# A side tile of dead scratch buffers for the weights between two attention layers

## The chip, the cores and the metric

The kernel runs on one core of one Trainium2 chip. The metric is the device time of one launch in microseconds, the median of several runs. Operand types are bf16, with f32 sums.

## The reference

One token is decoded for each of four sequences, through four layers: attention, gated linear unit (GLU), the same attention again, the same GLU again. The second pass uses the same caches and weights as the first.

```python
x = A_x                                             # [4, 1, 512]
x = x + _A_ref(_layernorm(x), k_cache, v_cache, wq, wo)
x = x + _B_ref(_layernorm(x), w_gate, w_up, w_down)
x = x + _A_ref(_layernorm(x), k_cache, v_cache, wq, wo)
x = x + _B_ref(_layernorm(x), w_gate, w_up, w_down)

# _A_ref: 32 query heads, 8 KV heads, Dh = 128; the window is the last 2048 keys (W = 8192 // 4)
q = (x @ wq)                                        # wq [512, 4096]
p = softmax(q k^T * Dh ** -0.5)
out = (p v).reshape(B, 1, 4096) @ wo                # wo [4096, 512]

# _B_ref: F = 1792
out = (sigmoid(x @ w_gate) * (x @ w_up)) @ w_down
```

The window's K and V are 16 MiB each, wq and wo 4 MiB each, the three GLU matrices 1.75 MiB each.

## The kernel before

**Space.** SBUF holds an arena of 50 slots of 128 x 2048 bf16 (512 KB a slot). Two slots are a tile: 1 MB, which holds one KV head of two sequences. The first 32 slots hold all of K and stay for both attention layers. The other 18 slots are nine tiles for V, wq, wo and the GLU weights. Beside the arena lie scratch buffers, each a tensor of its own: `prow` (the scores' exponentials P, 512 bf16), `ebuf` (P transposed, 512 f32, in halves for even and odd units, tokens `("e", 0)` and `("e", 1)`), `qh` and `qbd` (q, and q spread into blocks for the score products), `mxt`, `rinv`, `onb`, `onp`, and small constants and masks.

**Units.** An attention layer is eight units, one for each KV head h: scores (L872, L883), softmax (L893 to L915, exponentials on ScalarE), P turned by a permutation product and a VectorE transposition (`turn_p`, L922), PV (L960 in the first layer, L1041 in the second), and the output product with wo. The first layer goes through h = 0 to 7 and also transposes each K tile in place (L854); the second goes through h = 7 to 0.

**What is kept between the layers.** The second layer needs V again. V tiles are named (h, bp), where bp is the pair of sequences, and a V tile has two halves. Tile (7, 1) and tile (6, 1) stay in the arena (`stay`, L1427). Tile (7, 0) is moved to four PSUM banks (`stash`) and comes back into a free tile (`load_stash`). Of tile (6, 0) the second half stays (`KEPT`, `keep_half`, L626); its first half is loaded again for the second layer. Everything else of V is loaded again.

**The change of layers.** Between the two attention layers the GLU weights (12 loads) and wq again (8 half tiles) pass through six half-tile homes while K and the kept V stay in place. The homes are written down with the loads: `GB` is a free tile (two homes), `Y` the tile of V (7, 0) after its stash (two homes), `Z` the first half of V (7, 1)'s tile, whose content waits in PSUM meanwhile (`stash_half`, `unstash_half`), and `GA` the first half of V (6, 0)'s tile. A home is free when what was in it has been read. The second layer's wq goes in the order i = 1 (q heads of h = 4 to 7), then i = 0, four chunks each; the homes of the last two chunks of i = 0 later serve as scratch (`wide_buffers`).

```python
load_half(("wq", c, k, i), wq_d[:, c, i * SLOT:(i + 1) * SLOT], "bw_4k", SLOT,
          (((Y, 1), (GB, 0), (GB, 1), (GA, 0)), ((GB, 0), (GB, 1), (GA, 0), (Y, 0)))[i][c])
```

**Order.** All loads are issued by SyncE (SP) from one list, `loads`, in the list's order (helper `dma`, L395; all loads have line L398). A load waits on SP until the engines that use its buffer have finished, so a waiting load also holds those behind it. The work of each engine is put in order by a planner (`_schedule`) from estimated costs, and the dependencies are tokens, turned into semaphore waits by `_assign_sync`. From the first GLU's end on, TensorE's order is the program order (`P.chain = True`).

Names and lines for later steps: `load_half` L487, `bounds_of` L516 (rows of w_down in one load), `load_wq` L522, `load_glu` L554, `load_v` L609, `q_mms` L784 (q products, L795), `q_turn` L803 (writes all of `ebuf` and half of `qh`), `attn_first` L1171, `glu` L1305 (gate and up products L1342, first w_down products L1408, last ones L1383).

Of the kernel before, what the change touches and what calls it, by code (L numbers as in the profile page):

```python
# [6 lines left out]
F32 = mybir.dt.float32  # L7
# [271 lines left out]
def build(nc, A_x, A_k, A_v, A_wq, A_wo, B_wg, B_wu, B_wd, out, cfg=None):  # L279
# [42 lines left out]
    with es:  # L322
# [4 lines left out]
        prow = sb("prow", [128, 512], BF16)  # L327
        ebuf = sb("ebuf", [128, 512], F32)
        qbd = sb("qbd", [128, 2 * NB * 4 * NR], BF16)
        qh = sb("qh", [128, 2 * 64], BF16)  # L330
        eyew = sb("eyew", [128, 224], BF16)
        ones_f = sb("ones_f", [128, 32], F32)
        perm = sb("perm", [128, 128], BF16)
        sel_f = sb("sel_f", [128, NR], F32)
        sel_b = sb("sel_b", [128, NR], BF16)
        s3 = sb("s3", [128, 2 * 3], BF16)
        sres = sb("sres", [128, 2], F32)
        sel_r = sb("sel_r", [128, 2 * REP], F32)
        maskr = sb("maskr", [128, 32], F32)
        mxt = sb("mxt", [128, 2 * 32], F32)  # L340
        nmax = sb("nmax", [128, 6], F32)
        msk_s = sb("msk_s", [128, 32], BF16)
        msk_m = sb("msk_m", [128, 2], BF16)
        psm = sb("psm", [128, 2], F32)
# [4 lines left out]
        maskp = sb("maskp", [128, REP], F32)  # L349
        msks = sb("msks", [128, 22], F32)  # L350
# [4 lines left out]
        lnr = sb("lnr", [128, 2 * NB], F32)  # L355
        lnd = sb("lnd", [128, NB], F32)
        lnv = sb("lnv", [128, NB], F32)
        inv_d = sb("inv_d", [128, 1], F32)
        xn = sb("xn", [128, NX], BF16)
        hT = sb("hT", [128, NFC * NB], BF16)  # L360
        x_nat = prow[0:NB, 0:D]
        eg = qbd[:, 0:2 * NFC * NB].bitcast(F32)
        ident = ebuf[:, 0:64].bitcast(BF16)
        ps = es.enter_context(nc.psum_tensor("ps", [128, 8, 512], F32))
# [14 lines left out]

        def slot_ap(s):  # L380
            return arena[:, s * SLOT:(s + 1) * SLOT]

# [37 lines left out]
        GA = ("V", HKV - 2, 0, 0)  # L420
        KEPT = ("kept",)
        GB = ("pair",)
        base = {}
# [10 lines left out]
        def take_load():  # L434
# [9 lines left out]
            if name in (Y, Z, GA, GB):  # L444
                base[name] = s
# [41 lines left out]
        def load_half(name, src, rate, size, where_):  # L487
            left[name] = 1
            homes[name] = [where_]
            on_free[name] = lambda s: hfree.add(s)  # L490

            def emit(s):
                dma(str(name), slot_ap(s)[:, 0:size], src, w=[("slot", s)], rate=rate)
            loads.append((name, emit))
# [21 lines left out]
        def bounds_of(k):  # L516

            return [(a, min(NFC, a + 4)) for a in range(0, NFC, 4)] if k < NG else bounds[:-1] + [(bounds[-1][0], NFC - 2), (NFC - 2, NFC)]
# [3 lines left out]
        def load_wq(k):  # L522
# [3 lines left out]
            else:  # L526
                for i in (1, 0):
                    for c in range(NC):
                        load_half(("wq", c, k, i), wq_d[:, c, i * SLOT:(i + 1) * SLOT], "bw_4k", SLOT,
                                  (((Y, 1), (GB, 0), (GB, 1), (GA, 0)), ((GB, 0), (GB, 1), (GA, 0), (Y, 0)))[i][c])  # L530
# [23 lines left out]
        def load_glu(k):  # L554
            for nm, src in (("wg", wg_d), ("wu", wu_d)):
                if k == 0:
                    for c in range(NC):
                        load_half((nm, c, k), src[:, c, :], "bw_3k", F,
                                  (((GB, 0), (GB, 1), (GA, 0), (Y, 0)), ((Y, 1), (Z, 0), (GB, 0), (GB, 1)))[nm == "wu"][c])
# [3 lines left out]
            for (a, b) in bounds_of(k):  # L563
                if k == 0:
                    load_half(("wd", a, k), wd_d[:, a:b, :].rearrange("p k n -> p (k n)"), "bw_4k", (b - a) * D,
                              ((GA, 0), (Y, 0), (Y, 1), (Z, 0))[a // 4])
# [42 lines left out]
        def load_v(h, bp, k, n_use):  # L609
            name = ("V", h, bp, k)  # L610
            tiles = {(HKV - 2, 0): ((Y, 0),), (HKV - 3, 1): ((Y, 1), (GB, 0))}.get((h, bp)) if k else None
            if tiles is not None:
# [5 lines left out]
                if len(tiles) == 1:  # L618
                    halves[h, bp].append((KEPT, 0))
# [6 lines left out]
        def keep_half(s):  # L626
            hfree.add(s)
            where[KEPT] = s + 1
            left[KEPT] = 2
        on_free[GA] = keep_half  # L630

        P.op("gpsimd", "ones", 200.0, lambda g: g.memset(ones_f[:], 1.0), w=[("ones_f",)])
        P.op("gpsimd", "ident_b", 300.0,
# [9 lines left out]
        for jh in range(2):  # L643
            for bp in range(2):
                for i in range(2):
# [7 lines left out]
                         r=[("ones_f",), ("perm",)], w=[("perm", jh, bp, i)])  # L653
# [5 lines left out]
             r=[("ones_f",)], w=[("msk_s",)])  # L659
# [4 lines left out]
             r=[("ones_f",)], w=[("msk_m",)])  # L664
        P.op("vector", "sel_f", 200.0,
             lambda v: v.tensor_reduce(sel_f[:, :], perm[:, :].rearrange("p (g x) -> p x g", x=NR), AXX, ALU.add),
             r=perms, w=[("sel_f",)])
        P.op("gpsimd", "sel_b", 200.0, lambda g: g.tensor_copy(sel_b[:, :], sel_f[:, :]),
             r=[("sel_f",)], w=[("sel_b",)])
# [867 lines left out]
```

## Time and profile before

| What | Value |
|---|---|
| median of 3 runs | 178.61 us (178.54 to 178.78) |
| span of the profiled execution | 177.03 us |
| PE, DVE, ACT, POOL busy | 58%, 59%, 18%, 12% of the span |
| loads | 70.26 MB from HBM |
| DMA engines' time on them | 97.4% of 16 engines' span |
| rate, 12 to 92 us | 420 GB/s |
| rate, 104 to 118 us (GLU weights) | 404 GB/s |
| rate, 122 to 124 us (wq of the second layer) | 350 GB/s |
| second layer's first scores | from 126.2 us |
| last load lands | 174.2 us |

The profiled execution's own time is its span; what the timed runs have beyond it lies around the program's instructions. In the profile's pages PE is TensorE's matmul, PEld its weight load, DVE VectorE, ACT ScalarE, POOL GpSimd and SPq the queue of SyncE. A load is recorded with its issue and its landing; the trace also has the landing on each of the 16 DMA engines. Times are microseconds from the span's start.

### The profile page before, as it was taken

Reading aid. Unit: us, or ns where it says so; the run is one execution under the profiler, and the core shown is the slowest. Engines: PE = TensorE matmul, PEld = TensorE weight load, DVE = VectorE, ACT = ScalarE, POOL = GpSimd, SP = SyncE. Lnnn points to the kernel's source line nnn. Section 1 sums busy time; section 2 is a strip of 40 time slices with the busy share of each in tenths; the row PEclk is TensorE's granted clock in tenths of the full one; section 3 lists DMA queues with packets and bytes.
Section 4 is the critical chain, followed back from the end, with each engine's and each line's share of the span. In section 5 each row is a group of like instructions: output and inputs, shape, how many; then the busy total and the mean of one; then the engine's idle time right before and its main releaser. Section 6 shows DMA issues by size and latency. Waiting matters only on the chain.

```text
span 177.0 us, 3893 instructions
## 1 busy us (share of the span) xinstructions
PE 102.3 (58%) x1641; PEld 55.0 (31%) x1653; DVE 104.6 (59%) x256; ACT 32.7 (18%) x87; POOL 21.6 (12%) x88
## 2 busy tenths in 40 slices
PE   0536236382842634607418866456886999776663
PEld 0203112241431431603404852052323444435322
DVE  7307997838477375594383772304299999742351
ACT  2002031312030210300301101000043365430011
POOL 6100010101010100100100100000011454342000
PEclk9999999999999999999999999999999999975555
DMA  6999999999999999999999999999999999999980
GB/s 179 418 429 428 420 422 416 416 420 426 411 414 429 415 422 418 415 420 426 411 420 428 400 403 403 409 401 387 404 429 409 420 418 422 413 417 405 413 351 28
DMA packets 12882, 70.52 MB, mean 398 GB/s; under 512 B 1336, under 2 KB 1344, under 8 KB 6720
## 3 DMA queue, kind: packets, MB, share of 16 engines
q1 hardware_dynamic: 12856, 70.26, 97.4%
q8 instruction: 13, 0.21, 0.5%
q14 instruction: 5, 0.04, 0.1%
q10 hardware_dynamic: 8, 0.00, 0.0%
HBM read 70.26 MB, written 0.00 MB: 397 GB/s over the span
## 4 chain that ended last, share of the span: by engine, by line
DMA 38%; DVE 32%; PE 18%; issue 4%; SPq 4%; ACT 2%; DVEq 0%; ACTq 0%
DMA arena<-in_B_w_down_dram 15%; DMA arena<-in_A_v_cache_dram 15%; DVE arena L854 11%; PE ps L883 7%; DVE nmax L896 5%; DMA arena<-in_B_w_gate_dram 4%; DMA arena<-in_A_wq_dram 4%; SPq L398 4%; PE ps L973 3%; PE ps L872 2%; DVE nmax L900 2%; DVE mxt L904 2%; DVE ebuf L931 2%; PE ps L1162 2%; DVE arena L1064 2%
## 5 line engine op out<-in xcount | busy, mean ns | idle before, releaser
L854 DVE STREAM_TRANSPOSE arena<-arena 128x1024 f32<-128x1024 f32 x32 | 37.0, 1202 | 0.0
L883 PE MATMUL ps<-arena,qbd 128*32 128x512 bf16 x256 | 25.6, 537 | 0.0
L896 DVE TENSOR_REDUCE nmax<-ps 128x1 f32<-128x512 f32 x16 | 10.8, 675 | 19.4 <-PE ps L883 19.3
L973 PE MATMUL ps<-ebuf,arena 128*128 128x8 bf16 x576 | 17.7, 168 | 7.5 <-DMA arena<-in_A_v_cache_dram 4.4
L872 PE MATMUL ps<-msk_m,msk_s 128*32 128x512 bf16 x64 | 8.6, 526 | 23.1 <-DVE arena L854 21.8
L973 PEld LDWEIGHTS ps<-ebuf,arena 128*128 128x128 bf16 x576 | 16.8, 104 | 9.5 <-DMA arena<-in_A_v_cache_dram 5.5
L911 ACT ACTIVATE prow<-ps,nmax 128x512 bf16<-128x512 f32 x16 | 11.0, 687 | 35.1 <-DVE nmax L908 29.5
L847 ACT CAST qbd<-ps 128x256 bf16<-128x256 f32 x16 | 5.9, 370 | 45.0 <-PE ps L883 35.1
L940 POOL CAST s<-psm 128x1 bf16<-128x1 f32 x9 | 1.7, 187 | 84.0 <-ACT prow L911 84.0
L883 PEld LDWEIGHTS ps<-arena,qbd 128*32 128x32 bf16 x256 | 8.4, 121 | 10.4 <-issue 7.7
L795 PE MATMUL ps<-arena,xn 128*4 128x512 bf16 x64 | 8.5, 572 | 4.9 <-DMA arena<-in_A_wq_dram 4.4
L926 ACT CAST prow<-ps 128x512 bf16<-128x512 f32 x16 | 9.4, 585 | 9.9 <-PE ps L973 2.1
L1342 PE MATMUL ps<-arena,xn 128*4 128x448 bf16 x64 | 7.7, 547 | 4.2 <-DMA arena<-in_B_w_up_dram 1.9
L931 DVE STREAM_TRANSPOSE ebuf<-prow 128x256 f32<-128x256 f32 x16 | 7.0, 435 | 3.8 <-ACT prow L926 3.7
L872 PEld LDWEIGHTS ps<-msk_m,msk_s 128*32 128x32 bf16 x64 | 1.7, 98 | 24.1 <-DVE arena L854 22.7
L773 ACT ACTIVATE lnv<-ps 128x4 f32<-128x4 f32 x4 | 0.7, 173 | 41.0 <-PE ps L769 41.0
L1055 PE MATMUL ps<-arena,ebuf 128*32 128x512 bf16 x112 | 7.9, 405 | 0.2 <-DVE nmax L908 0.2
L842 PE MATMUL ps<-qh,eyew 32*128 32x64 bf16 x64 | 5.6, 217 | 3.7 <-ACT qbd L847 2.4
L807 DVE STREAM_TRANSPOSE ebuf<-ps 128x512 f32<-128x512 f32 x3 | 2.1, 717 | 9.4 <-PE ps L795 9.3
L1351 DVE STREAM_TRANSPOSE ebuf<-ps 128x448 f32<-128x448 f32 x4 | 2.6, 650 | 7.1 <-PE ps L1342 7.1
L1162 PE MATMUL ps<-onp,arena 128*128 128x16 bf16 x144 | 5.3, 175 | 2.5 <-DVE onp L996 2.2
L981 DVE TENSOR_TENSOR onb<-ps,rinv 128x16 bf16<-128x16 f32 x9 | 1.7, 185 | 8.3 <-PE ps L973 8.1
(112 smaller groups left out, 132.2 us busy)
## 6 DMA issues: line engine op xcount, KB each, us to landing
arena<-in_A_v_cache_dram SPq DMA_DIRECT2D x27, 1024.0 KB, 22.4
arena<-in_A_k_cache_dram SPq DMA_DIRECT2D x16, 1024.0 KB, 25.1
arena<-in_A_wq_dram SPq DMA_DIRECT2D x4, 1024.0 KB, 8.0
arena<-in_A_wq_dram SPq DMA_DIRECT2D x8, 512.0 KB, 6.2
arena<-in_A_wo_dram SPq DMA_DIRECT2D x3, 1024.0 KB, 26.2
arena<-in_B_w_down_dram SPq DMA_DIRECT2D x4, 512.0 KB, 6.4
arena<-in_B_w_gate_dram SPq DMA_DIRECT2D x4, 448.0 KB, 8.3
arena<-in_B_w_up_dram SPq DMA_DIRECT2D x4, 448.0 KB, 6.2
```

Source lines behind the costliest of these rows:

```text
L795: last = pe.matmul(ps[32 * hh:32 * hh + NB, qb, :], xn[:, c * NB:(c + 1) * NB], src[:, o + hh * 512:o + (hh + 1) * 512], start=(c == 0), s ...
L854: P.op("vector", "T%d_%d" % (h, t), c_dve(1024), lambda v, v32=v32: v.transpose(v32, v32), r=[("slot", 4 * h + t)], w=[("slot", 4 * h + t)])
L872: last = pe.matmul(ps[32 * gi:32 * gi + 32, bank, :], msk_s[:, :], msk_m[:, :].unsqueeze(1).broadcast_to([128, 256, 2]), start=True, stop= ...
L883: last = pe.matmul(ps[32 * gi:32 * gi + 32, bank, :], qbd[:, q0:q0 + 32], kt[:, cp // 2, cp % 2, jh * NJ:(jh + 1) * NJ, :], start=False, s ...
L896: lambda v: v.tensor_reduce(nmax[:, k2:k2 + 1], ps[:, bank, :], AXX, ALU.max),
L911: lambda a: a.activation(prow[:, :].rearrange("p (m x t) -> p m x t", x=32, t=2), ps[:, bank, :].rearrange("p (m t x) -> p m x t", x=32, t ...
L926: P.op("scalar", "pc" + tag, c_act(512), lambda a: a.copy(prow[:, :], ps[:, pb, :]), r=[("ppb", pb)], w=[("prow",)], banks=(pb,))
L931: P.op("vector", "pt" + tag, c_dve(256), lambda v: v.transpose(et, prow[:, :].bitcast(F32)), r=[("prow",)], w=[("e", k2)])
L973: last = pe.matmul(ps[:, ob, bp * 8:bp * 8 + 8], src[:, j * 128:(j + 1) * 128], ev[:, j % 2, j % 16 // 2, x0:x0 + 8], start=(j == 0), stop ...
L1055: last = pe.matmul(ps[32 * g:32 * g + 32, ob, :], ew[:, g, mq, t], src.rearrange("p (m t d) -> p t m d", t=2, d=128)[:, t], start=(n == 0) ...
L1162: last = pe.matmul(ps[:, WB, c * NR:(c + 1) * NR], tile_ap(s)[:, o + r_ * D + c * 128:o + r_ * D + (c + 1) * 128], ov[:, r_ * NR:(r_ + 1) ...
L1342: last = pe.matmul(ps[32 * g:32 * g + NB, gub[n], 0:NF], xn[:, c * NB:(c + 1) * NB], slot_ap(s)[:, g * NF:(g + 1) * NF], start=(c == 0), s ...
```

## The change

The scratch buffers `prow`, `qbd`, `qh`, `mxt` and `ebuf` become parts of one tensor, `side`, of 2560 bf16 columns. Its first 2048 columns are a half-tile home: P, q, q blocks and mxt in the first 1536 columns, and the first half of `ebuf` in the last 512. This home, `SP`, takes the place of `GA` between the layers. `stok` gives a load of it, and a product that reads it, the tokens of every buffer that lies in it; with loads of up to 1536 columns `ebuf` is left out. It is handed over in unit 6 of the first layer (`give(SIDE)`).

V (6, 0) now stays whole, so its first half is not loaded again. The homes of the other weights are shifted: wq's third chunk of i = 1 and one w_gate chunk go to `SP`, and wq's last chunk of i = 0 goes to Y's first half, where the V half used to go. w_down of the first GLU comes in loads of 3, 4, 4 and 3 rows, so that its first fits in 1536 columns. To make room, `hT` moves into `rinv`, `eg` into `onp`, two constants into `ebuf`, and the small tensors are packed into one; `one`, a single column of ones, is new.

```diff
-        prow = sb("prow", [128, 512], BF16)
-        ebuf = sb("ebuf", [128, 512], F32)
-        qbd = sb("qbd", [128, 2 * NB * 4 * NR], BF16)
-        qh = sb("qh", [128, 2 * 64], BF16)
+        side = sb("side", [128, 1536 + 1024], BF16)
+        prow, qbd, qh = side[:, 0:512], side[:, 512:512 + 2 * NB * 4 * NR], side[:, 1024:1024 + 2 * 64]
+        mxt = side[:, 1152:1152 + 4 * 32].bitcast(F32)
+        ebuf = side[:, 1536:1536 + 1024].bitcast(F32)
...
-        hT = sb("hT", [128, NFC * NB], BF16)
+        hT = rinv[:, 0:NFC * NB // 2].bitcast(BF16)
-        eg = qbd[:, 0:2 * NFC * NB].bitcast(F32)
+        eg = onp[:, 0:2 * NFC * NB].bitcast(F32)
...
+        SIDE = NS
+        side_toks = [("prow",)] + [(n, i) for n in ("q", "qh", "mk") for i in range(2)]
...
+        def stok(s, n=SLOT):
+            return [("slot", s)] + (side_toks if s == SIDE else []) + ([("e", 0)] if s == SIDE and n > 1536 else [])
...
-        GA = ("V", HKV - 2, 0, 0)
-        KEPT = ("kept",)
+        SP = ("side",)
+        base = {SP: SIDE}
...
-                dma(str(name), slot_ap(s)[:, 0:size], src, w=[("slot", s)], rate=rate)
+                dma(str(name), slot_ap(s)[:, 0:size], src, w=stok(s, size), rate=rate)
...
-            return [(a, min(NFC, a + 4)) for a in range(0, NFC, 4)] if k < NG else ...
+            return [(0, 3), (3, 7), (7, 11), (11, NFC)] if k < NG else ...
...
-    (((Y, 1), (GB, 0), (GB, 1), (GA, 0)), ((GB, 0), (GB, 1), (GA, 0), (Y, 0)))[i][c])
+    (((Y, 1), (GB, 0), (GB, 1), (Y, 0)), ((GB, 0), (GB, 1), (SP, 0), (Y, 0)))[i][c])
...
-    (((GB, 0), (GB, 1), (GA, 0), (Y, 0)), ((Y, 1), (Z, 0), (GB, 0), (GB, 1)))[nm == "wu"][c])
+    (((GB, 0), (GB, 1), (SP, 0), (Y, 0)), ((Y, 1), (Z, 0), (GB, 0), (GB, 1)))[nm == "wu"][c])
...
-              ((GA, 0), (Y, 0), (Y, 1), (Z, 0))[a // 4])
+              ((SP, 0), (Y, 0), (Y, 1), (Z, 0))[n])
...
-            tiles = {(HKV - 2, 0): ((Y, 0),), (HKV - 3, 1): ((Y, 1), (GB, 0))}.get((h, bp)) if k else None
+            tiles = ((Y, 1), (GB, 0)) if k and (h, bp) == (HKV - 3, 1) else None
...
+                if h == HKV - 2:
+                    give(SIDE)
...
-                 r=[("e", 0), ("e", 1), ("eg",), ("q", 0)], w=[("hT",)])
+                 r=[("e", 0), ("e", 1), ("eg",), ("op", 0), ("op", 1)], w=[("hT",)] + hts)
...
-        stay = keep[1:] + [(HKV - 2, 1)]
+        stay = keep[1:] + [(HKV - 2, 1), (HKV - 2, 0)]
...
-                    if n_v == cfg.get("ST", 2):
+                    if n_v == cfg.get("ST", 1):
```

## The prediction

> **What bounds the kernel now.** I read the page first: span, DMA rows, chain.
>
> ```profile
> span 177.0 us, 3893 instructions
> DMA  6999999999999999999999999999999999999980
> GB/s 179 418 429 428 420 422 416 416 420 426 411 414 429 415 422 418 415 420 426 411 420 428 400 403 403 409 401 387 404 429 409 420 418 422 413 417 405 413 351 28
> q1 hardware_dynamic: 12856, 70.26, 97.4%
> q8 instruction: 13, 0.21, 0.5%
> DMA arena<-in_B_w_down_dram 15%; DMA arena<-in_A_v_cache_dram 15%; DVE arena L854 11%; PE ps L883 7%; DVE nmax L896 5%; DMA arena<-in_B_w_gate_dram 4%; DMA arena<-in_A_wq_dram 4%; SPq L398 4%; PE ps L973 3%; PE ps L872 2%; DVE nmax L900 2%; DVE mxt L904 2%; DVE ebuf L931 2%; PE ps L1162 2%; DVE arena L1064 2%
> ```
>
> The 16 DMA engines are busy from the second slice to the last but two, at about 420 GB/s, and carry 70.26 MB of loads. The last 20.9 us of the chain are one w_down load waiting its turn in the queue. No engine is above 59%. So the time is the loads' bytes over their rate, plus what is lost where the queue runs low, plus some 3 us of tail. Where it runs low is in the windows (columns: stretch; PE, PEld, DVE, ACT, POOL busy; clock; DMA share; GB/s).
>
> ```profile
> 12.00:92.00 80.00, 36.69 (x624) 21.13 (x630) 53.60 (x95) 12.90 (x31) 5.28 (x28) 1.00 1.01 420
> 118.00:122.00 4.00, 2.81 (x26) 1.60 (x24) 2.39 (x8) 0.16 (x1) 0.00 (x0) 1.00 1.02 407
> 122.00:124.00 2.00, 1.09 (x8) 0.09 (x4) 0.16 (x1) 0.22 (x2) 0.00 (x0) 1.00 1.02 350
> 124.00:132.00 8.00, 6.92 (x68) 2.26 (x69) 4.51 (x11) 2.38 (x6) 0.15 (x1) 1.00 1.03 413
> 172.00:174.00 2.00, 1.41 (x48) 1.05 (x48) 0.00 (x0) 0.00 (x0) 0.00 (x0) 0.50 0.28 102
> ```
>
> Only 122 to 124 us falls clearly, to 350 GB/s: 2.00 x (1 - 350/420) = 0.33 us lost. The share stays at 1.02 there, so the rate tells of a low queue and the share does not. In 172 to 174 a quarter of the engines still move: some lag behind the others. Next, SP's queue around the change of layers, one row to a load, with its issue time:
>
> ```profile
> 120.56 0.33 SPq L398 DMA_DIRECT2D arena<-in_A_wq_dram  x1
> 121.27 0.33 SPq L398 DMA_DIRECT2D arena<-in_A_wq_dram  x1
> 122.54 0.33 SPq L398 DMA_DIRECT2D arena<-in_A_wq_dram  x1
> 123.83 0.54 SPq L398 DMA_DIRECT2D arena<-in_A_v_cache_dram  x1
> 125.11 0.54 SPq L398 DMA_DIRECT2D arena<-in_A_v_cache_dram  x1
> 126.45 0.54 SPq L398 DMA_DIRECT2D arena<-in_A_v_cache_dram  x1
> 128.16 0.54 SPq L398 DMA_DIRECT2D arena<-in_A_v_cache_dram  x1
> 130.62 0.54 SPq L398 DMA_DIRECT2D arena<-in_A_v_cache_dram  x1
> ```
>
> These are the last three wq halves (i = 0), the V half of (6,0), the two V halves of (5,1), and two whole V tiles. Each goes out when a buffer is read out, so the issue times are set by PE, not by DMA. The answers for single loads give size and microseconds to landing, here the very first load, the one issued at 120.56 and the one at 122.54:
>
> ```profile
> arena<-in_A_wq_dram SPq DMA_DIRECT2D x1, 1024.0 KB, 5.0
> arena<-in_A_wq_dram SPq DMA_DIRECT2D x1, 512.0 KB, 5.1
> arena<-in_A_wq_dram SPq DMA_DIRECT2D x1, 512.0 KB, 5.7
> ```
>
> The landings are then 125.68, 126.91, 128.19, 129.47, 130.76, 132.03, 134.53: 1.27 us a half tile, 2.49 us a tile. The last rows are PE's, which read out the buffers:
>
> ```profile
> 98.86 2.79 PE L973 MATMUL ps<-ebuf,arena 128*128 128x8 bf16 x96
> 117.45 1.04 PE L1408 MATMUL ps<-hT,arena 128*128 128x4 bf16 x24 [0.70 <-DMA arena<-in_B_w_down_dram]
> 123.19 0.60 PE L795 MATMUL ps<-arena,xn 128*4 128x512 bf16 x4 [0.69 <-DMA arena<-in_A_wq_dram]
> ```
>
> **The change, part by part.**
>
> *Removed: one 512 KB load,* the V half of (6,0) issued at 123.83. Everything behind it comes forward by its spacing, 1.27 us, if the queue stays fed. That is the whole possible saving.
>
> *The side tile takes its first load (wg, chunk 2) later.* Before, it went out at 99.88, when PV of unit 6 had read the first of its two tiles. Now it also waits for the second tile (P^T lies under it), for the transposition of unit 7's P and for its scores. Of the 96 matmuls in 2.79 us the first 64 are unit 6, so they end near 98.86 + 2 x 0.93 = 100.7; the P transposition ends at 99.02. Issue at 100.8, 0.9 us later. The load ahead lands at 106.76; with a start-up of 3.0 us (below) data would come at 103.8, 3 us early. The loads behind it on SP were issued at 101.68 and later. Cost 0; if that cover is gone, each microsecond of release past 103.8 costs one.
>
> *Down weights in 3, 4, 4, 3 rows, not 4, 4, 4, 2.* Same bytes. The last piece now has 12 matmuls after its landing, not 8: 4 x 0.59/16 = 0.15 us later to the residual, the layer norm and the first q products, so the wq halves issued at 120.56 and 121.27 move to about 120.7 and 121.4. These are the thinnest leads, 2.1 to 2.7 us ahead of the first engine that runs out, but the engines that lag finish the earlier load only at 124.42, so their order of landings does not move. Cost 0.05, at most 0.15.
>
> *The last wq half (i = 0, chunk 3) goes to Y's first half,* read by the q product of 123.19, which ends at 123.79; before it had GA's, read one product earlier. It is issued at 123.83 instead of 122.54. On SP the two V halves of (5,1) and the whole tiles stand behind it, but their own releases (125.11, 126.45, 128.16, 130.62) come later anyway. Its own reader, a q product behind the scores of the second unit, runs near 131, so PE does not wait. What it does cost is queue: the same issue times now have 1.27 us less work in front of them.
>
> So the term that decides is the start-up D from issue to flowing data. Lower end: the first load, 5.03 us for 2.49 us of data, D = 2.5. Upper end: the load of 120.56, 5.12 less 1.27 = 3.85, with part of that spent queueing. In between: the 0.33 us lost in 122 to 124. The engines finished the load before between 122.68 and 124.42 and took up the next between D = 2.2 and 3.5. I take 3.0. Following the last engine, where each load starts at the later of (landing before, issue + D):
> - wq half: from max(126.91, 126.83), lands 128.18
> - V halves: from max(128.18, 128.11), 129.45; from max(129.45, 129.45), 130.73
> - V tiles: from max(130.73, 131.16), 133.65; from max(133.65, 133.62), 136.14.
>
> Before, that last tile would have landed at 134.53 + 2.49 = 137.02. So 0.88 us of the 1.27 arrives; with D = 2.5 all of it (135.71, 1.3 us), with D = 3.85 none (136.99). After that tile, loads come in pairs (131.19, 134.15, ...) and the queue grows to 20 us, so what is won by 136 us is kept.
>
> The Trainium skill, "DMA: Bandwidth & Descriptors", Anatomy of one DMA, gives a fixed cost of about 2.0 us plus bytes over 436 GB/s. The first load here took 5.0 us where that gives 4.4; by the rule nothing would run dry and the sum would be 177.3.
>
> *Is the tail able to use it?* At the end wu's last half lands at 169.83 and its products start at 169.87; the ones before ended at 169.45, so 0.4 us of shift is free of any limit. Beyond it the products start at 169.47 whatever lands, hT is ready 171.75 - 0.4 = 171.35, and the first w_down load (172.33) may come 1.0 us earlier before it waits for hT; the last ones, 173.57 and 174.20, have 56 products of about 0.03 us from 171.35 on, over by 173.2, so 1.3 us fits.
>
> *The new aliases.* eg in onp waits for the output product of the last unit, done at 105.03 and needed at 110.61; hT in rinv for an operation of 103.2, needed at 114.88; ones and sel_f in ebuf for set-up operations over by 6.8, before the first q turn at 13.93. One memset of about 0.1 us comes first on POOL, and what it could delay stands before the q product of 7.30, while the queue is 20 us deep. All cost 0. The second wq load into the side tile waits for the down product of 115.25 (over at 115.7) as before, and the q turn that writes over it stands behind the products that read it. One V tile more comes free after unit 1; the queue is deep by then: 0.
>
> Sum: -1.27 + 0.39 (starved) + 0.0 to 0.05 = -0.85 to -0.9, so -0.9 us. The profiled span is 177.03; I expect 176.1. The median of the runs is 178.61, 1.58 more, lying around the span; that stays, so 177.7. The three runs lie within 0.24 us, so 0.2% (0.36 us) is about what can be told from no change.
>
> **Rivals.**
> - *All of it arrives.* D is 2.5, as the idle first load says, and 122 to 124 was slow for another reason: 178.61 - 1.3 = 177.3. For it: the wq halves of 121.27 and 122.54 have leads of 2.7 us on the fastest engine and the rate after 124 is 413. Against: 350 GB/s exactly behind the thinnest lead.
> - *All of it is eaten:* D near 3.8 for every engine, the loads of 128.16 and 130.62 start when they can and not when the queue allows: 178.6. Against: the two tiles issued at 128.16 and 130.62 had leads of 2.8 us and landed exactly 2.49 us behind the load before them.
> - *Slower: the side tile is handed over late.* If what the wg load waits for turns out to be the end of the layer (output product, 105.03) rather than 100.7, its data comes at 108.03 against 106.76, and all the loads stand 1.27 us behind it on SP: the saving is gone, the 0.39 us stays: 179.0. It decides from a release after 103.8, and the kernel is slower by 0.36 us from one after 105.0. For it: the tile has nine tokens on three engines. Against: each reader that I can place ends by 100.8.
> - *A fetch of instructions meets an engine that already lags.* q8's 13 packets take 0.5% of 16 x 177.03, 1.09 us each, on one engine each, and the final landing (174.20, most engines 172.7) is an engine that one held up. Two on the same engine: 177.7 + 1.1 = 178.8. Against: so far each of the four after 130 us made a new laggard. The Trainium skill, "Runtime: NRT & Kernel Launch", Instruction fetch mechanics, calls such a refill mostly hidden; the rows show it is not hidden from a saturated queue.
>
> **How the numbers follow.** Part of it arrives (gain 0.4 to 1.15): 0.56. All: 0.17. None: 0.10. Late hand-over: 0.12. Fetch: 0.05. Faster is the first two, 0.73; the same, none and fetch, 0.15; slower 0.12. The prediction is 177.7. The range runs from 177.2 (all, 0.1 for the runs' spread) to 178.6 (none); late hand-over and fetch, 0.17, lie outside. The likeliest case alone has 177.4 to 178.2.
>
> **What would show it.** HBM read 69.73 MB. The wg load issued near 100.8 with no dip in the rate between 104 and 110. The last wq half near 123.8, then V issues at unchanged times. A rate under 413 between 124 and 132; if it holds at 413, all of it arrived. Last landing near 173.3. The prediction is wrong if the issue times of V halves move by more than 0.3 us, or if the rate after 132 is not 416.

## The result and the profile after

| | before | after |
|---|---|---|
| median | 178.66 us (8 runs) | 179.56 us (8 runs, 179.0 to 180.33) |
| ratio | | 1.0051, 95% interval 1.0035 to 1.0068 |
| span of the profiled execution | 177.03 us | 178.1 us |
| last load lands | 174.20 us | 175.21 us |

The change makes the kernel 0.9 us slower; 0.9 us faster was predicted. The page of the changed kernel, its span, DMA rows and chain:

```profile
span 178.1 us, 3907 instructions
...
DMA  5999999999999999999999999999999999999990
GB/s 178 423 427 427 425 418 416 416 420 421 420 418 418 420 423 418 412 423 420 416 423 420 404 400 406 404 403 366 341 290 405 421 427 420 420 412 406 411 365 25
...
q1 hardware_dynamic: 12712, 69.74, 96.8%
...
DMA arena<-in_A_v_cache_dram 15%; DMA arena<-in_B_w_down_dram 13%; DVE arena L846 11%; PE ps L875 7%; DVE small L888 5%; DMA arena<-in_B_w_gate_dram 4%; DMA arena<-in_A_wq_dram 4%; SPq L398 4%; PE ps L965 3%; PE ps L864 2%; DVE small L892 2%; DVE arena L1056 2%; PE ps L916 2%; DVE side L896 2%; DVE side L923 2%
```

The bytes went as planned, 70.26 to 69.74 MB, and the chain ends in the same loads. But three slices of the rate, at about 120 to 134 us, now read 366, 341 and 290, where before they read 387, 404 and 429. No other slice lost anything like it. The windows of the changed kernel, with the columns of the prediction's (the last is GB/s, the one ahead of it the DMA share):

```profile
12.00:92.00 80.00, 39.38 (x630) 21.11 (x630) 53.57 (x95) 12.90 (x31) 5.28 (x28) 1.00 1.01 419
104.00:118.00 14.00, 7.50 (x96) 3.71 (x96) 4.41 (x15) 0.72 (x4) 0.00 (x0) 1.00 1.03 404
122.00:124.00 2.00, 1.04 (x8) 0.18 (x8) 0.00 (x0) 0.21 (x1) 0.00 (x0) 1.00 1.04 328
124.00:132.00 8.00, 7.31 (x73) 2.25 (x69) 4.31 (x11) 2.10 (x6) 0.00 (x0) 1.00 0.94 313
132.00:170.00 38.00, 30.93 (x466) 15.45 (x462) 26.36 (x87) 13.41 (x40) 11.81 (x35) 0.84 1.01 412
```

Against before (350, 413 and 416 in the last three), the changed kernel moves 2.00 x 22 + 8.00 x 100 = 844 KB less between 122 and 132 us, and 38 x 4 = 152 KB less until 170: 1.0 MB, 2.4 us at 420 GB/s. The removed 0.52 MB were worth 1.27 us. The difference, 1.1 us, is about what the last landing moved by (1.01). So most of the result, 844 of 996 KB, lies in these ten microseconds. SP's queue there, one row to a load, from the wq half of 120.56 before on:

```profile
120.59 0.33 SPq L398 DMA_DIRECT2D arena<-in_A_wq_dram  x1
121.23 0.33 SPq L398 DMA_DIRECT2D arena<-in_A_wq_dram  x1
124.19 0.33 SPq L398 DMA_DIRECT2D arena<-in_A_wq_dram  x1
125.45 0.54 SPq L398 DMA_DIRECT2D arena<-in_A_v_cache_dram  x1
126.82 0.54 SPq L398 DMA_DIRECT2D arena<-in_A_v_cache_dram  x1
128.53 0.54 SPq L398 DMA_DIRECT2D arena<-in_A_v_cache_dram  x1
131.09 0.54 SPq L398 DMA_DIRECT2D arena<-in_A_v_cache_dram  x1
```

The answers for the loads of 124.19, 125.45, 126.82 and 128.53 (size, microseconds to landing):

```profile
arena<-in_A_wq_dram SPq DMA_DIRECT2D x1, 512.0 KB, 4.9
arena<-in_A_v_cache_dram SPq DMA_DIRECT2D x1, 512.0 KB, 5.4
arena<-in_A_v_cache_dram SPq DMA_DIRECT2D x1, 512.0 KB, 6.1
arena<-in_A_v_cache_dram SPq DMA_DIRECT2D x1, 1024.0 KB, 7.4
```

They land at 129.09, 130.81, 132.96 and 135.93: spacings of 1.72 and 2.15 us for half tiles that took 1.27 before, and 2.97 for a tile that took 2.49. Count what is on the way at 128.0 us, issued and not landed: here three half tiles (of 124.19, 125.45 and 126.82); before four (of 122.54, 123.83, 125.11 and 126.45). How far this count explains the loss is what the later experiments are about.

### The profile page after: what moved, and what is told of

Its sections match the earlier page's. It is cut to its first block, busy times and chain, and to the rows that moved or that the text cites. A ratio compares the mean times of both kernels' runs of the same rounds, so it can differ in the third digit from the quotient of the medians.

```text
span 178.1 us, 3907 instructions
## 1 busy us (share of the span) xinstructions
PE 106.7 (60%) x1653; PEld 54.9 (31%) x1653; DVE 104.5 (59%) x256; ACT 32.7 (18%) x87; POOL 21.7 (12%) x89
## 3 DMA queue, kind: packets, MB, share of 16 engines
q1 hardware_dynamic: 12712, 69.74, 96.8%
## 4 chain that ended last, share of the span: by engine, by line
DMA 36%; DVE 33%; PE 20%; SPq 4%; issue 3%; ACT 3%; POOL 1%; DVEq 0%; ACTq 0%
DMA arena<-in_A_v_cache_dram 15%; DMA arena<-in_B_w_down_dram 13%; DVE arena L846 11%; PE ps L875 7%; DVE small L888 5%; DMA arena<-in_B_w_gate_dram 4%; DMA arena<-in_A_wq_dram 4%; SPq L398 4%; PE ps L965 3%; PE ps L864 2%; DVE small L892 2%; DVE arena L1056 2%; PE ps L916 2%; DVE side L896 2%; DVE side L923 2%
## 5 line engine op out<-in xcount | busy, mean ns | idle before, releaser
L875 PE MATMUL ps<-arena,side 128*32 128x512 bf16 x256 | 25.6, 537 | 0.0
L888 DVE TENSOR_REDUCE small<-ps 128x1 f32<-128x512 f32 x16 | 10.8, 675 | 19.5 <-PE ps L875 19.3
L864 PE MATMUL ps<-small,msk_s 128*32 128x512 bf16 x64 | 8.6, 526 | 22.4 <-DVE arena L846 21.8
L965 PE MATMUL ps<-side,arena 128*128 128x8 bf16 x576 | 17.8, 168 | 4.6 <-DMA arena<-in_A_v_cache_dram 4.5
L965 PEld LDWEIGHTS ps<-side,arena 128*128 128x128 bf16 x576 | 16.8, 104 | 9.8 <-DMA arena<-in_A_v_cache_dram 5.6
L903 ACT ACTIVATE side<-ps,small 128x512 bf16<-128x512 f32 x16 | 11.0, 687 | 35.2 <-DVE small L900 29.5
L916 PE MATMUL ps<-side,perm 128*128 128x512 bf16 x16 | 7.9, 496 | 7.5 <-ACT side L903 7.5
L875 PEld LDWEIGHTS ps<-arena,side 128*32 128x32 bf16 x256 | 8.4, 121 | 10.3 <-issue 7.7
L918 ACT CAST side<-ps 128x512 bf16<-128x512 f32 x16 | 9.4, 585 | 9.8 <-PE ps L916 9.8
L923 DVE STREAM_TRANSPOSE side<-side 128x256 f32<-128x256 f32 x16 | 7.0, 435 | 3.8 <-ACT side L918 3.7
L1047 PE MATMUL ps<-arena,side 128*32 128x512 bf16 x112 | 7.7, 396 | 0.1
```

The source lines that it names most:

```text
L864: last = pe.matmul(ps[32 * gi:32 * gi + 32, bank, :], msk_s[:, :], msk_m[:, :].unsqueeze(1).broadcast_to([128, 256, 2]), start=True, stop= ...
L875: last = pe.matmul(ps[32 * gi:32 * gi + 32, bank, :], qbd[:, q0:q0 + 32], kt[:, cp // 2, cp % 2, jh * NJ:(jh + 1) * NJ, :], start=False, s ...
L888: lambda v: v.tensor_reduce(nmax[:, k2:k2 + 1], ps[:, bank, :], AXX, ALU.max),
L903: lambda a: a.activation(prow[:, :].rearrange("p (m x t) -> p m x t", x=32, t=2), ps[:, bank, :].rearrange("p (m t x) -> p m x t", x=32, t ...
L916: lambda pe: pe.matmul(ps[:, pb, :], perm[:, :], prow[:, :], start=True, stop=True),
L918: P.op("scalar", "pc" + tag, c_act(512), lambda a: a.copy(prow[:, :], ps[:, pb, :]), r=[("ppb", pb)], w=[("prow",)], banks=(pb,))
```

## The experiments

Two theories at first. *Queue theory:* the half tile that was removed was what kept the DMA engines fed while the V halves waited for their homes, and without it the queue runs low for longer than 1.27 us. *Home theory:* the rearranged homes and the later gate on SP cost the time; removing the load is worth its 1.27 us. Medians stand against the kernel before in the same series, 178.57 to 178.64 us. In `skip` one half of V (6, 0) is not used and the other is used twice, so its output is another; the kernels that load something again load the same data onto itself.

**refill**, the changed kernel with the removed bytes put back behind wq:

```diff
...
         load_wq(1)
+        load_half(("again",), pair_d(A_v, HKV - 2, 0)[:, :, 0:SLOT], "bw_4k", SLOT, (GA, 0))
```

> The changed kernel with 512 KB more: the first half of V (6,0) is loaded once more onto itself, behind wq, with nothing to wait for but its place in SP's order. Queue theory (the removed load was what the DMA engines worked on until the tile released by the second layer's first scores could arrive, issue 128.5 plus some 4 us): the gap between 127 and 133 us closes, the rate there is back near 410 GB/s, and the time is that of the kernel before or a little over it, 178.6 to 179.0 us, although more is loaded. Home theory (the side tile and the later home of the last wq half cost the time by themselves): nothing gets faster, and 1.27 us of load comes on top of 179.56, 180.5 to 180.8 us.

Measured 179.41 us, ratio 1.0037 (1.0006 to 1.0068). The 1.27 us of loading that were added cost nothing against 179.56. Home theory falls; queue theory is not fully met either, as the time does not come back to 178.6.

**skip**, the kernel before with that one load removed and nothing else changed: old homes, old w_down rows, no side tile.

```diff
+                if len(tiles) == 1:
+                    halves[h, bp] = [(KEPT, 0), (KEPT, 0)]
+                    return
```

> The kernel before, without the second load of V (6,0)'s first half; no side tile, all homes and lines as before. It leaves out that load, and PV of this unit reads the half that stayed twice, so the output is not the reference's. Queue theory: the same gap opens before the tile released at 128.2 us, and nothing or less than nothing is saved, 178.5 to 179.3 us. Home theory: without side tile and without a later home the whole load is saved, 177.3 to 177.7 us.

Measured 179.36, ratio 1.0038 (1.0017 to 1.0058): taking a load away, alone, makes the kernel 0.7 us slower. Its windows:

```profile
122.00:124.00 2.00, 0.87 (x8) 0.09 (x4) 0.40 (x1) 0.02 (x1) 0.00 (x0) 1.00 1.00 356
124.00:132.00 8.00, 7.30 (x73) 2.30 (x77) 4.51 (x12) 2.38 (x6) 0.39 (x2) 1.00 0.97 326
```

The side tile and the shifted homes are not needed to make the hole.

**gate**, the kernel before with two homes exchanged, so that the last wq half waits for Y's first half (as in the changed kernel) and the V half of (6, 0) for `GA`; all bytes stay. **swap**, the changed kernel with `SP` and Y's first half exchanged in every stage, so that this wq half goes out at 122.27 again.

```diff
 gate:
-  (((Y, 1), (GB, 0), (GB, 1), (GA, 0)), ((GB, 0), (GB, 1), (GA, 0), (Y, 0)))[i][c])
+  (((Y, 1), (GB, 0), (GB, 1), (Y, 0)), ((GB, 0), (GB, 1), (GA, 0), (Y, 0)))[i][c])
-            tiles = {(HKV - 2, 0): ((Y, 0),), ...
+            tiles = {(HKV - 2, 0): ((GA, 0),), ...
 swap:
-  (((Y, 1), (GB, 0), (GB, 1), (Y, 0)), ((GB, 0), (GB, 1), (SP, 0), (Y, 0)))[i][c])
+  (((Y, 1), (GB, 0), (GB, 1), (Y, 0)), ((GB, 0), (GB, 1), (Y, 0), (SP, 0)))[i][c])
...
-              ((SP, 0), (Y, 0), (Y, 1), (Z, 0))[n])
+              ((Y, 0), (SP, 0), (Y, 1), (Z, 0))[n])
```

> The kernel before with all its loads, the homes of two of them exchanged: the last wq half goes to Y's first half (issued near 123.8 us instead of 122.5), the V half of (6,0) to GA's, right behind it. Queue theory: the V half fills the queue, the cost is at most the 0.3 us by which the late half starves the first engines, 178.6 to 179.0 us. Home theory with the late wq half as the culprit: 179.4 us or more.

> The changed kernel with the side tile and Y's first half exchanged in all three stages (gate weights, down weights in 4, 3, 4, 3 rows, wq), so that the last wq half is issued behind the third q product again (near 122.6 us instead of 124.2). Queue theory: one of the two causes of the gap is gone, the other (no load between 122.6 and the V half at 125.3) stays: 178.6 to 179.3 us, better than the changed kernel by 0.2 to 0.9 us and not under the kernel before by more than 0.2. Home theory: the saving appears, 177.6 to 178.0 us.

gate: 179.01, ratio 1.0017 (0.9993 to 1.0042), no clear difference. swap: 179.50, ratio 1.0054 (1.0032 to 1.0077), no better than the changed kernel, though its wq half went out 1.9 us earlier than 124.19; both theories had it faster. The rate from 124 to 132 us is 329 GB/s in swap. So the later gate is not needed for the loss; by itself it costs less than 0.8 us, the upper end of gate's interval.

**halves**, the changed kernel with V (5, 0) and V (4, 1) as two half loads each, so that the first half could start when its own slot is free:

```diff
+            if k and (h, bp) in ((HKV - 3, 0), (HKV - 4, 1)):
...
+                    for n in range(2):
+                        dma("%s_%d" % (name, n), slot_ap(s + n), pair_d(A_v, h, bp)[:, :, n * SLOT:(n + 1) * SLOT],
+                            w=[("slot", s + n)], rate="bw_4k")
```

> The changed kernel with the first two whole V tiles of the second layer, (5,0) and (4,1), each issued as two half-tile loads into the same tile. Start-up theory (from an empty queue a V tile's data flows some 3.9 us after its issue, a half's some 2.9 us): V (5,0) begins about 1 us earlier, the gap before 133 us shrinks, 178.6 to 179.1 us. If start-up is the same for both sizes and the gap comes only from the missing load: 179.3 to 179.8 us.

Measured 180.17, ratio 1.008 (1.0051 to 1.011), above the changed kernel's 179.56 and outside both expectations. Halves that start earlier gain nothing; the rate from 124 to 132 is 334.

**turn**, the kernel before with two homes changed, so that the sixth wq half goes out at 118.25 and not at 120.56; **turnkeep**, swap with the same two homes; **turnkeephalves**, both with the half loads.

```diff
 turn:
-  (((Y, 1), (GB, 0), (GB, 1), (GA, 0)), ((GB, 0), (GB, 1), (GA, 0), (Y, 0)))[i][c])
+  (((Y, 1), (GB, 0), (GB, 1), (GA, 0)), ((Z, 0), (GB, 1), (GA, 0), (Y, 0)))[i][c])
...
-              ((GA, 0), (Y, 0), (Y, 1), (Z, 0))[a // 4])
+              ((GA, 0), (Y, 0), (Y, 1), (GB, 0))[a // 4])
```

> The kernel before with two homes exchanged and nothing else: the last down load goes to GB's first half and the first wq half to Z, so that the sixth wq half waits for a down product (near 118.1 us) and no longer for the first q product (120.56). Lead theory (what is lost is lost where loads are issued less than some 3 us before the engines run out): the dip to 350 GB/s at 122 to 124 us goes, 178.2 to 178.5 us. Home theory (homes cost nothing by their lead): the same time, 178.5 to 178.7 us.

> The kernel of the exchange of side tile and Y's first half, with the same two homes exchanged as in the last run; V (6,0) stays whole. Lead theory: wq arrives without a dip, but the hole where the V half was issued stays, and V (5,0) can't come sooner than its issue plus its start-up: 178.6 to 179.2 us. Home theory: 177.5 to 178.0 us.

> The last kernel, and V (5,0) and (4,1) issued as half-tile loads as well. Start-up theory: V (5,0) starts some 1 us sooner, part of the saved load arrives, 178.0 to 178.5 us, below both the kernel before and the changed one. If start-up is the same for both sizes: like the last kernel, 178.6 to 179.2 us.

turn: 178.91, ratio 1.0007 (0.9985 to 1.0028). The rate in 122 to 124 rises from 350 to 371 and from 124 to 132 it is 400; the time shows no clear difference. turnkeep: 180.05, ratio 1.0066 (1.0043 to 1.0089), 367 and 295 GB/s in the same windows. turnkeephalves: 181.41, ratio 1.0125 (1.0088 to 1.0163). Filling the dip ahead of the hole does not close the hole. All three medians lie above the ranges of both theories. Why the half loads make it worse, most of all together with turnkeep, stays open.

**early** and **early256**, the changed kernel with 512 KB or 256 KB loaded again ahead of the last wq half, not behind it; **big**, as refill with both halves; **split**, the kernel before with w_down in 3, 4, 4 and 3 rows.

```diff
 early, early256 (SLOT // 2):
...
+                        if i == 0 and c == NC - 1:
+                            load_half(("again",), pair_d(A_v, HKV - 2, 0)[:, :, 0:SLOT], "bw_4k", SLOT, (GA, 0))
 split:
-            return [(a, min(NFC, a + 4)) for a in range(0, NFC, 4)] if k < NG else ...
+            return [(0, 3), (3, 7), (7, 11), (11, NFC)] if k < NG else ...
...
```

> The changed kernel with one 512 KB load more (the first half of V (6,0) again, onto itself), now ahead of the last wq half and not behind it as in refill; its result is not used. Bytes are those of the kernel before. Empty-queue theory: what counts is that a load stands in the queue at 122 to 124 us, when the last wq half cannot be issued yet (124.2); this one can be issued near 122, the engines do not run dry, and the time is that of the kernel before, 178.6 to 178.9. Theory of the other edits (side tile, aliases, w_down rows cost 0.7 us by themselves, since refill at 179.41 did not come back to 178.6): 179.3 to 179.6.

> As early, with 256 KB in place of 512 KB. Empty-queue theory: 0.63 us less to move than in early and half of the cover, so between 178.2 (cover is still enough) and 179.1 (half of the hole comes back). Theory of the other edits: 178.7 to 179.6, following the bytes: early less 0.63, or no change from early.

> The changed kernel with both halves of V (6,0) loaded again onto themselves behind the last wq half (1 MB; refill had 512 KB there); their results are the same data. Empty-queue theory: the changed kernel loses about 2.4 us of moving between 122 and 134 us and refill filled half of it at no cost; the second half megabyte fills most of what is left, 179.4 to 180.0. If the time lost is not time in which the queue had nothing to move, each added half tile costs its 1.27 us: refill's 179.41 + 1.27 = 180.7.

> The kernel before with w_down of the first layer in loads of 3, 4, 4 and 3 rows, nothing else changed. The prediction's term: at most 0.15 us, 178.6 to 178.75. Rival: the last w_down product ends later and the wq halves that wait for it are the ones with the thinnest lead, so a dip in the rate at 122 to 124 us deepens: 179.0 to 179.3.

early: 178.85, ratio 1.0021 (1.0003 to 1.0038). With the same bytes as refill, put where a load can go out while the last wq half still waits (121.40 us), its median is 0.6 us under refill's (their intervals overlap). In its profiled execution, its fastest at 178.46, most of the hole is gone:

```profile
122.00:124.00 2.00, 0.86 (x8) 0.09 (x4) 0.41 (x1) 0.01 (x1) 0.00 (x0) 1.00 1.04 361
124.00:132.00 8.00, 6.83 (x73) 2.22 (x77) 4.51 (x12) 2.38 (x6) 0.40 (x3) 1.00 1.00 403
```

So with the bytes back at this place all the other edits together (side tile, aliases, gates, w_down rows) cost 0.05 to 0.7 us; with skip, the greater part of the loss is the missing load. early256: 179.74, ratio 1.0063 (1.0041 to 1.0085). That is outside what either theory gave (queue theory at most 179.1): in its six runs half a cover gained nothing.

split: 179.02 over 12 runs, ratio 1.0032 (1.0006 to 1.0059), so 0.1 to 1.05 us for an edit that was priced at 0.05 and at most 0.15. The rival's mechanism shows, weakly: the rate at 122 to 124 is

```profile
122.00:124.00 2.00, 0.96 (x8) 0.09 (x4) 0.33 (x1) 0.11 (x1) 0.00 (x0) 1.00 1.00 328
```

where before has 350. The profiled execution took 178.65 us, under the median, and shows no more than that; of the longer ones there is no trace.

big: 181.20, ratio 1.0147 (1.0134 to 1.016), against the queue theory's 179.4 to 180.0. The second half megabyte costs 1.8 us more than refill, above its 1.27, so the other reading (180.7) is also missed. Its window and the load issued at 126.20:

```profile
124.00:132.00 8.00, 7.07 (x73) 2.27 (x77) 4.52 (x12) 2.38 (x6) 0.41 (x3) 1.00 1.00 344
```

```profile
arena<-in_A_v_cache_dram SPq DMA_DIRECT2D x1, 512.0 KB, 9.2
```

A queue that simply runs empty does not explain this: six half tiles are on the way on average, the share is 1.00, loads wait 9 us, and the rate is 344. In the trace, 44% of the 4 KB packets that start between 129 and 132 us in big take over 200 ns; undisturbed they take 159 ns, and before has 3% of such packets from 124 to 130. The theory "empty or not" does not fit big and early256. Three of the next four runs measure directly how the rate depends on what is on the way.

**infl2, infl3, infl4** load the K of heads 0 to 2 as twelve half tiles, each waiting for the landing of the half tile two, three or four ahead of it, early in the kernel, so that two, three or four are on the way. **hole** makes the first K load wait once for the fourth wq tile, with a deep list of 1 MB loads behind it.

```diff
 infl2 (3, 4):
...
+                for k in range(2):
+                    late = tok(where["wq", 3, 0])[:1] if s + k < 2 else [("slot", s + k - 2)]
+                    dma("K%d_%d_%d" % (h, bp, k), slot_ap(s + k), pair_d(A_k, h, bp)[:, :, k * SLOT:(k + 1) * SLOT],
+                        r=late, w=[("slot", s + k)], rate="bw_4k")
 hole:
+                late = tok(where["wq", 3, 0])[:1] if h + bp == 0 else []
```

> The kernel before with the K loads of heads 0 to 2 as twelve half tiles, each of which waits for the landing of the second half tile ahead of it: two in flight. The rate between about 17 and 40 us by start-up alone: a half tile every (D + 1.27)/2, so D = 2.4 gives 1.84 us, 286 GB/s; the prediction's 3.0 gives 2.14 us, 246 GB/s. If a thin queue also has slow packets, it is below 246.

> As infl2 with three half tiles in flight. By start-up alone: a half tile every max(1.27, (D + 1.27)/3): D = 2.4 gives 1.27, full rate (413 to 420 GB/s); the prediction's 3.0 gives 1.42 us, 369. If a thin queue also has slow packets: 300 to 350, as in the second layer of gate and refill.

> As infl2 with four half tiles in flight. By start-up alone: full rate for every D up to 3.8 (413 to 420 GB/s). If an interruption or a thin queue leaves packets slow by itself: below 380.

> The kernel before, with one interruption early in the first layer: the first K load waits until the fourth wq tile has landed (13.2 us), with the whole deep list of 1 MB loads behind it. All the work is done. If any interruption leaves the stream slow, the rate stays near 300 GB/s for some 4 us after the loads start again (near 16 us); if slowness needs a thin queue, the rate is 420 at once and the loss is the hole alone, start-up less 0.5 us, 2 to 3.3 us.

These four were run once each: 198.66, 190.97, 185.50 and 181.15 us, with 179.76 for the kernel before in the same series. The same window of infl2, infl3 and infl4, one fence each:

```profile
18.00:27.00 9.00, 0.00 (x0) 0.00 (x0) 2.88 (x3) 0.00 (x0) 0.00 (x0) 1.00 0.67 211
```

```profile
18.00:27.00 9.00, 0.00 (x0) 0.00 (x0) 2.49 (x2) 0.00 (x0) 0.00 (x0) 1.00 0.89 299
```

```profile
18.00:27.00 9.00, 0.00 (x0) 0.00 (x0) 3.74 (x3) 0.00 (x0) 0.00 (x0) 1.00 1.02 392
```

211, 299 and 392 GB/s with two, three and four half tiles on the way. The start-up model of the prediction (D = 3.0) gave 246, 369 and full rate; D = 2.4 gave 286 and full rate twice. Both are too fast, by a sixth to over a third at two and three. The third reading, slow packets as well, fits two (below 246), just misses three (300 to 350) and misses four (below 380). A half tile (524 KB in thousands of bytes) takes 2 x 524 / 211 = 5.0 us from issue to landing with two on the way, 5.3 with three and with four. So, carried a little beyond what was run, about 413 x 5.3 / 524 = 4.2 half tiles have to be on the way for the full rate.

hole, the windows across and behind the interruption:

```profile
13.00:16.00 3.00, 2.04 (x15) 0.95 (x16) 1.84 (x4) 0.76 (x3) 0.00 (x0) 1.00 0.44 142
16.00:20.00 4.00, 0.74 (x8) 0.43 (x8) 2.00 (x3) 0.37 (x1) 0.00 (x0) 1.00 1.01 424
```

Against the trace of before, hole is 1.05 MB behind at 90 us as at 30 us, 2.5 us at 420 GB/s (its span is 2.4 us longer; the single times differ by 1.4). So one interruption costs its own length, once, and the rate is 424 at once when a deep list stands behind it. An interruption by itself leaves nothing slow.

With this the second layer can be read as a count. Mean half tiles issued and not landed from 126 to 129 us, worked out from the loads' issue and landing times, with the rate (GB/s) in these and the next three microseconds:

| kernel | half tiles on the way, 126 to 129 | rate, 126 to 129 | rate, 129 to 132 |
|---|---|---|---|
| before / split / early | 4.4 / 4.5 / 4.5 | 406 / 407 / 386 | 421 / 415 / 414 |
| turn | 4.4 | 399 | 395 |
| early256 | 3.9 | 373 | 355 |
| skip / changed / swap | 3.5 / 3.5 / 3.5 | 339 / 313 / 362 | 257 / 261 / 244 |
| turnkeep / halves / turnkeephalves | 3.5 / 3.3 / 3.3 | 337 / 326 / 355 | 183 / 298 / 220 |
| gate / refill | 4.6 / 4.6 | 347 / 365 | 329 / 351 |
| big | 5.8 | 374 | 274 |

From 126 to 129 us the first five rows lie within some 35 GB/s of the line that infl3 and infl4 give (299 at three, 392 at four). The count does not give the whole loss, though. From 129 to 132 us the kernels without the load fall far below that line, although by then 4 to 5 half tiles are on the way in each (some issued less than 3 us before). More than half of what the changed kernel misses from 122 to 132 us lies there, 480 of 844 KB.

The packets show part of what happens. In skip the first twelve 8 KB packets of V (5, 0), from 129.68 us on, take 0.77 to 1.88 us each, against 0.31 for most of the later ones. In the changed kernel the first nine, from 130.35 on, take 0.96 to 2.10. In before the first sixteen take at most 0.33. So time goes at the start of the first whole tile, and it is recorded as busy time. That the engines had run out of work there is likely, but the trace does not tell which engine moved a packet.

The last two rows do not fit: gate, refill and big have enough on the way from 126 us on and are still some 40 to 65 GB/s under the full rate, and further under it from 129 us on. (gate's profiled execution took 179.78, over its median.) All three had only 3.7 on the way from 122 to 124 us (before 4.4). Why packets stay slow for some 5 us after that, though enough is queued by then, is open; hole shows it is not interruption alone. The 16 engines also run up to 1.7 us apart within one load (122.68 to 124.42 in before), and no run holds them together.

Nor does the count explain the dip of before itself: 4.4 on the way from 122 to 124, and 350 GB/s. Two of those had been issued little more than 2 us ahead of the first engine that took them up (120.56 against 122.68), less than the 2.9 of a half tile alone. This suggests that both matter, the count and the lead. What the runs settle is that taking this load away costs 0.7 us by itself; the count goes with the first part of the loss, and the cause of the rest is open.

## Why the prediction was wrong

- *Removed load, -1.27 us, "if the queue stays fed".* The bytes and the spacing were right. The condition failed, and skip shows it by itself: the removal alone is +0.7 us.
- *The step that failed:* the term that decides, "each load starts at the later of (landing before, issue + D)" with D = 3.0. It lost 0.39 us; 2.2 us were lost by the medians (1.27 + 0.90), 2.4 by the rates. D itself was not far off: a half tile alone on idle engines lands after 4.2 to 4.4 us (the first K halves of infl2 to infl4), 1.27 of it data, so 2.9 to 3.1. What failed is to let everything behind the start flow at full speed, one load behind the other. With the changed kernel's own issue times the rule puts the V halves at 129.82 and 131.09 and V (5, 0) at 134.02; they landed 0.99, 1.87 and 1.91 us later. Moved issue times explain 134.02 - 133.65 = 0.37 us of the miss at this tile. In place of full speed the runs show 299 GB/s with three half tiles on the way (infl3), and 326 from 124 to 132 us in skip. Why packets get that slow stays open.
- *Reading the dip of 122 to 124.* "The share stays at 1.02 there, so the rate tells of a low queue and the share does not" took the dip for late starts. In before 13% of the 4 KB packets that start in this window take over 200 ns, against 3% in the six microseconds behind it: packets were on the way, and slow. That does not rule out late starts, as a start shows as slow packets too: in infl2's first two half tiles 81% of the packets from 14.4 to 15.2 us take over 200 ns, and 8% of those from 16.0 to 18.4. What was wrong is to price the dip at 0.33 us and take it for all that a shorter queue can cost.
- *The lead in before* was counted in microseconds ahead of one engine; by infl2 to infl4 half tiles on the way count as well, and before had 4.4 where some 4.2 are needed. By that there was no room to take one away.
- *Last wq half at 123.83:* 124.19, and the V halves 0.34 and 0.37 us later than before, over the 0.3 that was named as a sign of error. The third wq half landed at 122.25 and not at 121.86, as one engine was 0.45 us behind the other fifteen. A fetch of instructions at 119.06 took 0.88 us and is likely what held it, though the trace does not name its engine. By the Trainium skill, "Runtime: NRT & Kernel Launch", Instruction fetch mechanics, such a refill is mostly hidden; if that is the cause, this one was not. It is not what decides: in skip the V halves went out at 124.84 and 126.22, earlier than before, and it is slow all the same.
- *Side tile, cost 0:* right. wg was issued at 100.75 (100.8 predicted) and the rate from 104 to 118 us is 404 in both kernels. The rival of a late hand-over did not happen.
- *w_down rows, 0.05 to 0.15 us:* mis-sized. The residual moved by 0.03 us in the trace of the changed kernel, but split measures 0.57 us (0.1 to 1.05) for the edit, and why it is so much the runs don't settle: the windows show only the deeper dip at 122 to 124. This and the removal (skip, 0.68) make 1.25, against 0.9 (0.6 to 1.2) for the whole change.
- *New aliases, 0:* with the bytes back, early bounds all edits but the load count to 0.05 to 0.7 us, and split alone has 0.57. Nothing points to the aliases, but no run prices them by themselves.
- *Tail:* nothing came early enough to try it.
- *Two slips in the working.* The tile issued at 130.62 did not land "exactly 2.49 us behind the load before": before's views give it 7.7 us, so 138.34, 3.8 us behind. Fifteen engines were done with it at 137.02 and one was 1.3 us later, so against "all of it is eaten" only the tile of 128.16 stands. And the sum is -0.83 to -0.88, not -0.85 to -0.9. Neither decides the miss.
- *Rivals.* "All of it is eaten" had the place of the loss, and ended at 178.6 because its rule could lose no more than was saved. "All of it arrives" rested on D = 2.5 from the idle first load of 1 MB; half tiles alone give 2.9 to 3.1. The Trainium skill, "DMA: Bandwidth & Descriptors", Anatomy of one DMA, has a rule that would give the same time: a fixed cost of about 2.0 us, plus bytes over 436 GB/s. That section of the Trainium skill states it for loads that GpSimd issues, and these are issued by SyncE. A half tile alone took 4.2 to 4.4 us where the rule gives 3.2, and for two half tiles on the way an estimate by it is 1.05 MB in 2.0 + 1.2 us, 328 GB/s; infl2 has 211. The measurement decides.

## What to carry to other kernels

Where loads are issued just in time, count the half tiles (or bytes) issued and not landed, beside the microseconds of lead. In infl2 to infl4, 512 KB halves moved at 211, 299 and 392 GB/s with two, three and four on the way; by extension some 4.2 (2.2 MB) are needed for the full rate here. The count is a warning and not a full account: gate, refill and big were slow with more. Removing a load from such a stretch takes a buffer's worth of cover away, and can cost more than its bytes save (skip, 0.7 us). By this account bytes are to be removed where the queue is deep, which was not tried here. A DMA share of 1.0 does not show that the engines move data at full speed: packets that take many times their usual 159 or 309 ns count as busy.

## What was unexpected

- Fewer bytes, slower kernel: 0.52 MB less, 0.7 us more (skip), and 0.52 MB more at another place 0.7 us back (early, 178.85, against 179.56).
- Place may matter as well as size: the same 512 KB gave 178.85 when issued at 121.40 and 179.41 when issued behind the last wq half; 256 KB at the first place gave 179.74. The intervals of the first two overlap.
- With few loads on the way single 4 KB packets slow down: over 200 ns for 22%, 15% and 6% of them in infl2, infl3 and infl4 (159 ns undisturbed), although the DMA engines are not all busy (share 0.67 in infl2).
- An interruption in front of a deep queue costs its own 2.5 us of loading and nothing after it.
